# Moving four of the last output-projection products behind the last V pair, and splitting the copy of the last output half between ScalarE and VectorE

## The chip, the cores and the metric

One core of one Trainium2 chip. The metric is the device time of one execution in microseconds (us), median of several runs; lower is better. "Span" is the time from the first to the last instruction in a profile; the device time is some 2 us longer.

## The reference, cut to what matters

One decode step of an attention block over a KV cache, mixed by a gate with a small feed-forward block.

```python
B, Sq, D = 4, 1, 1024;  H, Sk, Dh = 32, 8192, 128        # all bf16
q = (x @ wq) ...                                          # [B, H, 1, Dh]
p = softmax(einsum("bhqd,bhkd->bhqk", q, k_cache) * Dh ** -0.5)
o = einsum("bhqk,bhkd->bhqd", p, v_cache)
a = o.reshape(B, Sq, H * Dh) @ wo                         # wo: 4096 x 1024, 8 MB
b = x + (silu(x @ w_gate) * (x @ w_up)) @ w_down * sigmoid(x @ w_r)   # one token per batch
out = g * a + (1 - g) * b                                 # g = sigmoid(sum(x * gate_w)), out: 4 x 1024
```

The two caches are 268 MB each and everything is read once, so the kernel is one long read from HBM.

## The kernel before: the parts that matter

Heads are taken in 32 "pairs" of 8 MB, `d = 0..31`. All loads go through one ring of five 4 MB slots and are issued by SyncE (SP), in program order. The end of the program is what the change touches: the last V pair (`d = 31`), the eight 1 MB blocks of `wo`, and the output.

```python
def v_pair(d):                                     # cut
    ...                                            # the last pair comes in pieces: 2 x 2 MB, 4 x 1 MB
    for u in range(4 * RD):                        # 64 products of 512 columns
        for w in range(4):
            nc.tensor.matmul(o_ps[w // 2][row:row + NM, w % 2, :], ...)      # L579
    if tv == GV - 1:
        sum_up(d, g, t, b, h0)

def sum_up(d, g, t, b, h0):                        # cut: the branch for the last pairs
    half = [OS[:], turned(P, 4 * Dh, F32)]
    for w in range(2):
        nc.scalar.activation(out=half[w], in_=o_ps[0][:, w, :], ...)         # L615
    for w in range(2):
        nc.vector.scalar_tensor_tensor(out=half[w], in0=o_ps[1][:, w, :], ...)   # L617
    nc.vector.tensor_tensor(out=OS[:], in0=half[0], in1=half[1], op=ALU.add)     # L619
    # finish(), run later: 8 small products that transpose OS into "led"     # L625

def wo_block(g, r0=0, r1=FR, half=None):           # issues the load, returns the products
    ...
    nc.sync.dma_start(out=w[:, r0:r1]..., in_=wov[:, g, r0:r1]...)           # L432
    def use():
        for r in range(r0, r1):
            for n in range(NH) if half is None else [half]:
                mm_acc(n, LT[:, r, g, :], w[:, r, n * NB:(n + 1) * NB])      # L287, 512 columns
    return use

# the end of the program
        if (kind, d) == ("v", ND - 1):
            for g in range(2):
                wo_block(g)()                      # 16 products ahead of the last V pair
        if kind == "v":
            v_pair(d)
        if (kind, d) == ("v", ND - 2):
            o_rows(0, GE)                          # LT for the wo blocks up to GE
last = [wo_block(g) for g in range(2, 4)]
cuts = [(g, r, r + 2) for g in range(4, NWB - 1) for r in (0, 2)] + [(NWB - 1, r, r + 1) for r in range(FR - 1)] + [(NWB - 1, 3, 4, n) for n in range(NH)]
last += [wo_block(*cut) for cut in cuts]
flush_sums()
last.pop(0)()                                      # block 2
flush()                                            # the transposing products of the last pair (L625)
flush_late()
last.pop(0)()                                      # block 3
o_rows(GE, NWB)                                    # L419, L421
for use in last:                                   # blocks 4 to 7, in ever smaller pieces
    use()
res = [turned(Bn, NB) for _ in range(NH)]
nc.vector.tensor_copy(out=res[0], in_=acc(0))      # L684
nc.sync.dma_start(out=out2[:, 0:NB], in_=res[0])   # L685
nc.scalar.copy(out=res[1], in_=acc(1))             # L686
nc.scalar.dma_start(out=out2[:, NB:D], in_=res[1]) # L687
```

## Time and profile before

| | before |
|---|---|
| device time, first three runs | 1342.71, 1342.55, 1342.71 us |
| span | 1340.5 us |
| HBM read | 575.68 MB |
| last V piece landed | 1321.86 us |
| last wo piece landed | 1337.07 us |
| last wo product starts | 1337.12 us |
| last arrival of the output | 1339.45 us |

A transfer has landed when the last of its increments is in (16 for a load; the small output transfers show five); I read those times from the semaphore records of the trace. The lines that carry the reading are in the prediction; one more, the last V pair, which runs its 64 products without a wait:

```profile
1310.84 14.00 PE L579 MATMUL o_ps<-ring,PB 128*64 128x512 bf16 x64
```

How to read the lines: in a chain, "start, length, what"; in a timeline, the same with engine, source line and operation, and in brackets how long the engine was idle before and for whom it waited. PE is TensorE, PEld its weight loads, DVE VectorE, ACT ScalarE, SPq and ACTq the issue of a transfer by SyncE or ScalarE.

### The profile page before, as it was taken

Reading aid. Unit: us, or ns where it says so; the run is one execution under the profiler, and the core shown is the slowest. Engines: PE = TensorE matmul, PEld = TensorE weight load, DVE = VectorE, ACT = ScalarE, POOL = GpSimd, SP = SyncE. Lnnn points to the kernel's source line nnn. Section 1 sums busy time; section 2 is a strip of 40 time slices with the busy share of each in tenths; the row PEclk is TensorE's granted clock in tenths of the full one; section 3 lists DMA queues with packets and bytes.
Section 4 is the critical chain, followed back from the end, with each engine's and each line's share of the span. In section 5 each row is a group of like instructions: output and inputs, shape, how many; then the busy total and the mean of one; then the engine's idle time right before and its main releaser. Section 6 shows DMA issues by size and latency. Waiting matters only on the chain.

```text
span 1340.5 us, 6937 instructions
## 1 busy us (share of the span) xinstructions
PE 1065.4 (79%) x4654; PEld 141.1 (11%) x1422; DVE 638.4 (48%) x385; ACT 57.7 (4%) x58; POOL 66.5 (5%) x174
## 2 busy tenths in 40 slices
PE   2666877887778788787879778789697879889888
PEld 0101000001001010101001010101011011111111
DVE  2455988556544347554436256646145556100001
ACT  0000000100010000100010000100000000110000
POOL 2000000100010000100010000100001000100000
PEclk9787999898988998888989888889898989889889
DMA  9999999999999999999999999999999999999998
GB/s 415 433 436 435 437 434 427 435 432 430 437 433 429 441 427 427 440 432 432 437 431 431 432 437 438 425 432 427 438 436 438 430 422 434 434 430 429 428 427 346
DMA packets 15512, 576.14 MB, mean 430 GB/s; under 512 B 1740, under 2 KB 2004, under 8 KB 3170
## 3 DMA queue, kind: packets, MB, share of 16 engines
q1 hardware_dynamic: 15474, 575.69, 99.6%
q8 instruction: 24, 0.39, 0.1%
q14 instruction: 6, 0.05, 0.0%
q10 hardware_dynamic: 8, 0.00, 0.0%
HBM read 575.68 MB, written 0.01 MB: 429 GB/s over the span
## 4 chain that ended last, share of the span: by engine, by line
DMA 60%; DVE 23%; PE 14%; another core or an unknown queue 1%; issue 0%; ACT 0%; SPq 0%; DVEq 0%
DMA ring<-in_A_k_cache_dram 51%; DVE TB L494 21%; PE o_ps L579 9%; DMA ring<-in_A_v_cache_dram 8%; PE acc L287 2%; PE S_ps L499 2%; DVE OS L609 2%; DMA x<-in_gate_w_dram 2%; DVE mx L521 0%; PE o_ps L333 0%; PE S_ps L333 0%; PE led L625 0%; DVE PT L535 0%; ACT TB L530 0%
## 5 line engine op out<-in xcount | busy, mean ns | idle before, releaser
L494 DVE STREAM_TRANSPOSE TB<-ring 128x2048 uint32<-128x2048 uint32 x256 | 568.2, 2278 | 471.6 <-DMA ring<-in_A_k_cache_dram 464.6
L499 PE MATMUL S_ps<-TB,Z 128*128 128x512 bf16 x2048 | 531.3, 414 | 187.3 <-DVE TB L494 179.7
L579 PE MATMUL o_ps<-ring,PB 128*64 128x512 bf16 x2048 | 466.4, 390 | 45.7 <-DMA ring<-in_A_v_cache_dram 44.4
L499 PEld LDWEIGHTS <-Z 128*128 128x128 bf16 x512 | 52.9, 103 | 650.7 <-issue 650.7
L579 PEld LDWEIGHTS <-PB 128*64 128x64 bf16 x512 | 57.5, 112 | 447.0 <-issue 442.6
L617 DVE SCALAR_TENSOR_TENSOR OS<-o_ps,mE,OS 128x512 f32<-128x512 f32 x5 | 3.8, 751 | 136.7 <-ACT OS L615 136.7
L476 POOL COPY Z<-qa 32x4 bf16<-32x4 bf16 x128 | 25.6, 200 | 720.4 <-PE S_ps L499 695.0
L555 POOL COPY PB<-PT 32x1024 bf16<-32x1024 bf16 (+3 forms) x23 | 33.2, 1443 | 455.5 <-PE o_ps L579 350.1
L605 ACT ACTIVATE OS<-o_ps,mE 128x512 f32<-128x512 f32 x11 | 7.6, 687 | 673.4 <-PE o_ps L579 673.4
L553 ACT COPY PB<-PT 32x1024 bf16<-32x1024 bf16 (+3 forms) x21 | 30.3, 1442 | 22.5 <-PE o_ps L579 17.5
L609 DVE SCALAR_TENSOR_TENSOR OS<-o_ps,mE,OS 128x512 f32<-128x512 f32 x33 | 24.3, 737 | 1.5
L530 ACT ACTIVATE TB<-S_ps,mx 128x2048 bf16<-128x2048 f32 x4 | 7.9, 1967 | 321.4 <-DVE mx L527 321.4
L287 PE MATMUL acc<-ring,hT 128*4 128x512 bf16 x54 | 14.7, 444 | 5.4 <-ACT TB L530 5.4
L245 PE MATMUL S_ps<-identb,x 6*128 6x6 bf16 x8 | 0.6, 197 | 22.1 <-DMA x<-in_gate_w_dram 22.1
L333 PE MATMUL o_ps<-ring,xw 128*4 128x512 bf16 (+2 forms) x128 | 13.1, 496 | 5.2 <-DMA ring<-in_B_w_gate_dram 5.2
L287 PE MATMUL acc<-ring,LT 128*4 128x512 bf16 x64 | 14.6, 379 | 0.4 <-DVE LT L421 0.4
L625 PEld LDWEIGHTS o_ps<-selg,OS 128*128 128x128 f32 x88 | 11.5, 191 | 9.3 <-issue 8.9
L535 DVE STREAM_TRANSPOSE PT<-TB 128x2048 bf16<-128x2048 bf16 x4 | 9.2, 2312 | 6.4 <-ACT TB L530 6.4
L521 DVE TENSOR_REDUCE mx<-S_ps 128x1 f32<-128x2048 f32 x4 | 9.1, 2282 | 6.2 <-PE S_ps L499 6.2
L625 PE MATMUL o_ps<-selg,OS 128*128 128x8 f32 x88 | 10.5, 245 | 0.0
L615 ACT ACTIVATE OS<-o_ps,mE 128x512 f32<-128x512 f32 x5 | 3.4, 687 | 149.3 <-PE o_ps L579 149.3
L637 DVE SCALAR_TENSOR_TENSOR OT<-led,sgb,rinv 128x8 bf16<-128x8 f32 x5 | 1.2, 237 | 17.3 <-PE led L625 17.3
(83 smaller groups left out, 89.0 us busy)
## 6 DMA issues: line engine op xcount, KB each, us to landing
ring<-in_A_v_cache_dram SPq DMA_DIRECT2D x18, 4096.0 KB, 28.9
ring<-in_A_k_cache_dram SPq DMA_DIRECT2D x14, 4096.0 KB, 33.5
ring<-in_A_v_cache_dram SPq DMA_DIRECT2D x6, 2048.0 KB, 36.8
ring<-in_B_w_gate_dram SPq DMA_DIRECT2D x1, 7168.0 KB
ring<-in_B_w_up_dram SPq DMA_DIRECT2D x1, 7168.0 KB, 37.0
ring<-in_B_w_down_dram SPq DMA_DIRECT2D x1, 6912.0 KB
ring<-in_A_wo_dram SPq DMA_DIRECT2D x4, 1024.0 KB, 32.5
ring<-in_A_v_cache_dram SPq DMA_DIRECT2D x4, 1024.0 KB, 36.0
```

The costliest lines, as they stand in the source:

```text
L287: nc.tensor.matmul(acc(n), lhsT=lhsT, rhs=rhs, start=start, stop=True, skip_group_check=True)
L333: nc.tensor.matmul(ps[32 * k:32 * k + Bn, z, :].rearrange("p (f r) -> p f r", r=FR)[:, :, lo:hi], lhsT=xT[TW * half + t], rhs=rhs, start=( ...
L476: nc.gpsimd.tensor_copy(out=Z[at, :, QP - 1 + QP * q], in_=qa[at, :, h0 + q, b])
L494: nc.vector.transpose(out=flat_t.bitcast(U32).rearrange("p (j i) -> p j i", j=CJ), in_=kn[:, half].bitcast(U32))
L499: nc.tensor.matmul(sps[:, z, :], lhsT=Z[:, 2 * half + e, s:s + P], rhs=T[:, 16 * z:16 * z + 16, :, e], start=(t + n + half + e == 0), stop ...
L521: nc.vector.tensor_reduce(out=mx[:, 0:1], in_=sps[:].rearrange("p z n -> p (z n)"), axis=AX.X, op=ALU.max)
L535: nc.vector.transpose(out=PT[:].rearrange("p j i -> p (j i)"), in_=PTs)
L553: nc.scalar.copy(out=Bv[at, :, :, q, :], in_=Pv[at])
L555: nc.gpsimd.tensor_copy(out=Bv[at, :, :, q, :], in_=Pv[at])
L579: nc.tensor.matmul(o_ps[w // 2][row:row + NM, w % 2, :], lhsT=PB[:, RD * (d % NW) + n, z].rearrange("p w s j -> p (w s j)"), rhs=vn[:, j0 ...
L609: nc.vector.scalar_tensor_tensor(out=OS[:], in0=o_ps[w // 2][:, w % 2, :], scalar=mE[:, w:w + 1], in1=OS[:], op0=ALU.mult, op1=ALU.add)
L625: nc.tensor.matmul(oT, lhsT=OS[:, q * Dh:(q + 1) * Dh], rhs=selg[:, q].rearrange("p t s -> p (t s)"), start=(q == 0), stop=(q == 3), skip_ ...
```

## The change

The intent: fill the gap in which TensorE waits for the sums of the last V pair, with products that until then stood ahead of that pair; and let two engines share the copy of the output half that is ready last.

```diff
-        def use():
-            for r in range(r0, r1):
+        def use(lo=r0, hi=r1):
+            for r in range(lo, hi):
...
         if (kind, d) == ("v", ND - 1):
-            for g in range(2):
-                wo_block(g)()
+            wo_block(0)()
+            near = wo_block(1)
+            near(0, 2)
+            last = [lambda: near(2, FR)]
...
-    last = [wo_block(g) for g in range(2, 4)]
+    last += [wo_block(g) for g in range(2, 4)]
...
-    last.pop(0)()
+    for _ in range(2):
+        last.pop(0)()
...
-    res = [turned(Bn, NB) for _ in range(NH)]
+    NC = NB // 2
+    res = [turned(Bn, NB) for _ in range(3)]
     nc.vector.tensor_copy(out=res[0], in_=acc(0))
     nc.sync.dma_start(out=out2[:, 0:NB], in_=res[0])
-    nc.scalar.copy(out=res[1], in_=acc(1))
-    nc.scalar.dma_start(out=out2[:, NB:D], in_=res[1])
+    nc.scalar.copy(out=res[1][:, 0:NC], in_=acc(1)[:, 0:NC])
+    nc.vector.tensor_copy(out=res[2][:, 0:NC], in_=acc(1)[:, NC:NB])
+    nc.scalar.dma_start(out=out2[:, NB:NB + NC], in_=res[1][:, 0:NC])
+    nc.sync.dma_start(out=out2[:, NB + NC:D], in_=res[2][:, 0:NC])
```

## The prediction

> **What bounds the kernel now.** I began with the page, to see which resource is full from end to end.
>
> ```profile
> PE 1065.4 (79%) x4654; PEld 141.1 (11%) x1422; DVE 638.4 (48%) x385; ACT 57.7 (4%) x58; POOL 66.5 (5%) x174
> DMA  9999999999999999999999999999999999999998
> HBM read 575.68 MB, written 0.01 MB: 429 GB/s over the span
> ```
>
> No engine is full, but the DMA row is at nine tenths or more in 39 of 40 slices, so the kernel is a stream of 575.68 MB from HBM with compute beside it. A change at the end can only pay if it shortens what comes after the last bytes, or brings those bytes earlier. So the second view was the chain of waits, cut to the last 34 us.
>
> ```profile
> 1307.29 3.62 PE acc L287 x16
> 1310.91 13.51 PE o_ps L579 x62
> ...
> 1326.61 0.70 DVE OS L619
> 1327.31 0.04 issue
> 1327.35 1.06 PE led L625 x8
> 1328.41 1.82 PE acc L287 x8
> ...
> 1330.40 6.02 PE acc L287 x27
> 1336.42 0.04 issue
> 1336.46 1.05 PE acc L287 x4
> 1337.51 0.02 issue
> 1337.53 0.57 ACT TB L686
> ```
>
> Read alone, this says TensorE all the way: 16 wo products, the last V pair, ScalarE and VectorE summing it, the products that transpose the sum (L625), the other wo products, a copy. That reading invites the change. But a chain goes through the predecessor on the same engine when an engine hardly pauses, and can hide that a transfer paces it: the 0.04 us "issue" at 1336.42 is a small break. So I read TensorE's matmuls and weight loads, and the DMA issues, in order of time.
>
> ```profile
> 1327.35 1.06 PE L625 MATMUL led<-selg,OS 128*128 128x8 f32 x8 [0.70 <-DVE OS L619]
> 1334.75 0.08 PEld L287 LDWEIGHTS <-LT 128*4 128x4 bf16 x1 [0.38 <-issue]
> ...
> 1336.67 0.08 PEld L287 LDWEIGHTS <-LT 128*4 128x4 bf16 x1 [0.55 <-issue]
> 1328.21 0.33 SPq L432 DMA_DIRECT2D ring<-in_A_wo_dram  x1
> 1337.30 0.68 DVE L684 CAST TB<-acc 4x512 bf16<-4x512 f32 x1 [6.64 <-PE acc L287]
> 1337.53 0.57 ACT L686 CAST TB<-acc 4x512 bf16<-4x512 f32 x1 [11.82 <-PE acc L287]
> 1338.01 0.29 SPq L685 DMA_DIRECT2D out_dram<-TB  x1
> 1338.13 0.54 ACTq L687 DMA_DIRECT2D out_dram<-TB  x1
> ```
>
> The first line is the gap that the change aims at: TensorE waits for OS (0.70 us after the modelled end of the product before it; from issue to issue 0.86). Next come the weight loads, normally 0.35 us apart here; two gaps are longer, 0.38 and 0.55, and belong to products that wait for a wo piece. The piece issued at 1328.21 (the third row of the last block) has this landing time:
>
> ```profile
> ring<-in_A_wo_dram SPq DMA_DIRECT2D x1, 256.0 KB, 8.2
> ```
>
> 1328.21 + 8.2 = 1336.41, and the product that needs it starts at 1336.46. So the end is paced by DMA. In the trace's semaphore records, each of these transfers is complete when the last of 16 arrivals is in: first half of block 4 at 1328.15, second 1329.43; block 5 at 1330.70 and 1331.99; block 6 at 1333.25 and 1334.49; block 7 row by row at 1335.11, 1335.75, 1336.41, and its last row in halves at 1336.78 and 1337.07. Half a block comes every 1.25 us or so; its four products take 4 x 0.216 = 0.86 us. TensorE is faster than the stream and had caught up with it already at 1334.53, where it first had to wait (landing 1334.49).
>
> **What the Trainium skill says.** "TensorE: Matmul & The Clock Gate", section "Back-to-back issue gap", gives N/2.4 + 2.5 ns, 216 ns at N = 512; here successive products are 0.216 us apart, so it agrees, and I use 0.216. "VectorE: DVE Perf Modes", section on the TRN2 errata, gives PSUM to SBUF copies (120 + N)/0.96 ns on VectorE and (172 + N)/1.2 ns on ScalarE: 658 and 570 ns at N = 512, against 678 and 574 in the lines above. So the slopes hold, and a 256-column copy should take 678 - 256/0.96 = 411 ns on VectorE and 574 - 256/1.2 = 361 ns on ScalarE (estimates from that page and these rows). "PSUM — Partial Sum Buffer", section "PSUM bank collisions raise a hardware error", says two engines may not be on the same bank and quadrant at once, disjoint columns included, and that the compiler orders such instructions. The trace of before has one engine per bank here and can't show it, but the built order of the changed kernel does: VectorE's second copy waits for ScalarE. "DMA: Bandwidth & Descriptors", section "Anatomy of one DMA", puts some 2.0 us of fixed cost on a transfer, mostly completion. Measured here, from the issue's start to the last arrival: 1338.01 to 1339.28 and 1338.13 to 1339.45, so 1.27 us on SyncE's queue and 1.32 on ScalarE's. I use the measured ones.
>
> **The change, part 1: four products moved.** Nothing is added or removed on TensorE. Four of the eight products of wo block 1 go from ahead of the last V pair to behind it, 4 x 0.216 = 0.86 us.
> - The last V pair starts at about 1309.98 instead of 1310.84, if its data are there. They are: its first piece landed at 1307.02. The tightest is its last quarter, landed at 1321.86; its first product was the 57th, at 1310.84 + 56 x 0.216 = 1322.94, and would be at 1322.08. The slack falls from 1.08 to 0.22 us and just holds.
> - ScalarE and VectorE then sum 0.86 us earlier: OS is ready at 1327.31 - 0.86 = 1326.45.
> - The moved four products, then block 2's eight, fill TensorE to 1326.49: the gap is filled almost exactly, and L625 starts at 1326.5 instead of 1327.35. This is a real 0.85 us at that place.
> - Then the pieces. Block 3 (landed 1326.87) runs at about 1327.5 to 1329.2, the last output rows' products until 1329.3, block 4 at 1329.3 and 1330.2, block 5's first half at 1331.05 (landed 1330.70). Its second half could start at 1331.9 but lands at 1331.99: wait. Block 6 could start at 1332.9, lands at 1333.25: wait; its second half could start at 1334.15 and starts, as before, at 1334.53. From there on the two kernels coincide. The 0.85 us becomes three waits for DMA instead of one gap for VectorE.
>
> Do the pieces land earlier? Their issues wait for the transfer eight places ahead (SyncE's queue waited for transfers in all of its last issues), the order on SyncE is unchanged, and the DMA share is 1.0 until 1330. So no. Part 1: 0.0 us.
>
> **Part 2: the output.** Before: ScalarE copies the second half from 1337.53 to 1338.10, issues at 1338.13, last arrival 1339.45. After:
> - VectorE's first copy is unchanged, 1337.30 to 1337.98; its transfer lands at 1339.28.
> - ScalarE copies 256 columns, 1337.53 to 1337.89, and its transfer lands at 1337.92 + 1.32 = 1339.24: 0.21 earlier.
> - VectorE's second copy must wait for its own first (1337.98 at the latest) and for ScalarE (1337.89 + 0.03). Start about 1337.95, + 0.41 = 1338.36; SyncE issues at 1338.39, being free since 1338.30; + 1.27 = 1339.66.
> The last arrival is now this one: 1339.66 against 1339.45, 0.2 us later. The balance was meant to be better, but VectorE is the engine that is still busy with the other half, so it is given work that it starts 0.42 us after ScalarE could. The buffers of their own only avoid a false dependence that was not there.
>
> Sum: 0.0 + 0.2. 1342.71 + 0.2 = 1342.9.
>
> **The rivals.**
> 1. TensorE really sets the end and the 0.85 us carries through: 1342.71 - 0.85 + 0.2 = 1342.1. For it: the chain names TensorE alone. Against it: the start at 1336.46, 0.05 us after a landing.
> 2. The output copy gains what it was meant to: two queues issue in parallel and half copies are shorter, so the end follows ScalarE's 1339.24 or the untouched 1339.28, about -0.17: 1342.5. For it: VectorE's two neighbouring sums start 0.67 apart at 0.75 us each, so neighbours overlap by some 0.08. Against: even so the last half can't be copied before 1338.3.
> 3. The last V pair catches up with its data and TensorE stalls: the slack is only 0.22 us. Even a stall of 0.5 us leaves TensorE ahead of where it must be at 1334.53, so still 1342.9.
> 4. A collision or queue effect on the third output transfer, a second one on SyncE's queue: some 0.3 us more, 1343.2.
>
> **Range and chances.** All terms together lie between -0.85 and +0.5 us, and the three runs of before lie within 0.16 us. Runs of another session may shift by some tenths, so 1342.1 to 1343.6. Two per cent is 27 us, which nothing here can reach: within 2% is all but certain.
>
> **What would show it.** In the changed kernel's trace: L625 of the last pair starting about 0.85 us earlier with no idle ahead of it; longer gaps than 0.35 us between weight loads from block 5 on; the product on the third row of the last block still 0.05 us behind its landing; the second VectorE copy ending near 1338.36 and its transfer the last to land. Wrong would be: the last wo product earlier by more than 0.3 us with landings as they were, or the third output transfer landing before ScalarE's.

## The result, and the profile after

1343.09 us median of five runs (1342.89 to 1343.96), against 1342.71 us (1342.55 to 1342.99) for before: 0.38 us slower, the ratio 1.0004 with a 95% interval of 0.999 to 1.0018. Ratios are the mean time of one kernel's runs over that of the other's of the same rounds, so not quite the ratio of the medians. The number lies in the forecast range, and there is no gain, as forecast. The trace says which steps held.

The chain of waits of the changed kernel, last 34 us:

```profile
1307.61 21.05 DMA ring<-in_A_wo_dram
...
1328.72 8.19 DMA ring<-in_A_wo_dram
1336.91 0.04 issue
1336.96 0.82 PE acc L287 x3
1337.78 0.02 issue
1337.80 0.68 DVE TB L688
1338.48 0.35 DVE TB L691
```

Now the chain names what paced the end: two wo transfers, one after the other, and TensorE only for the last products. The third row of the last block landed at 1328.72 + 8.19 = 1336.91, the product that needs it started at 1336.96: the 0.05 us of before. This is no new bottleneck: in before the last 31 products took 7.10 us, against 6.85 without a wait (e12 below), so TensorE already lost 0.25 us to late pieces, in pauses too short for the chain to leave the engine.

The timeline of the changed kernel, the lines of the last V pair (L579), the transposing products and the wo products with a wait:

```profile
1307.88 3.64 PE L579 MATMUL o_ps<-ring,PB 128*64 128x512 bf16 x16
1312.48 7.07 PE L579 MATMUL o_ps<-ring,PB 128*64 128x512 bf16 x32 [0.97 <-DMA ring<-in_A_v_cache_dram]
1319.93 1.89 PE L579 MATMUL o_ps<-ring,PB 128*64 128x512 bf16 x8 [0.38 <-DMA ring<-in_A_v_cache_dram]
1322.42 1.89 PE L579 MATMUL o_ps<-ring,PB 128*64 128x512 bf16 x8 [0.60 <-DMA ring<-in_A_v_cache_dram]
1326.92 1.06 PE L625 MATMUL led<-selg,OS 128*128 128x8 f32 x8
1333.79 1.02 PE L287 MATMUL acc<-ring,LT 128*4 128x512 bf16 x4 [0.22 <-DMA ring<-in_A_wo_dram]
1335.01 2.98 PE L287 MATMUL acc<-ring,LT 128*4 128x512 bf16 x12 [0.20 <-DMA ring<-in_A_wo_dram]
```

The idle time ahead of L625 is gone and waits for wo pieces have come, as forecast. But the waits in the second to fourth line were not forecast: the last V pair waits for its own data. TensorE came to it at 1307.88 us, 2.96 us earlier than in before, and only 0.86 of that is the four products moved. The rest is, by the estimate below the windows, the clock. The same stretch of both kernels by windows (columns: stretch, its length, busy us of PE, PEld, DVE, ACT, POOL with instructions, granted TensorE clock, DMA share, GB/s), before first:

```profile
1285.00:1300.00 15.00, 12.47 (x43) 2.97 (x17) 1.25 (x3) 0.00 (x0) 0.00 (x0) 0.66 0.99 419
```

```profile
1285.00:1300.00 15.00, 11.94 (x52) 2.37 (x20) 0.24 (x1) 0.00 (x0) 0.00 (x0) 0.89 0.99 417
```

In before the clock was at half for 10.24 us from 1285.6, in the run of after for 3.41 us from 1287.4. The pair ahead of the last was then multiplied, at 0.43 us a product instead of 0.216, for 8.36 us of the stretch in before and 2.80 in after. Half of the difference is 2.78 us; less the 0.53 by which that pair began later in after, this estimate gives 2.25, where 2.10 are to be explained. The program is the same up to there, and either order had both lengths (below, 3.4 us in e6 in the old order and 10.2 in e7 in the new), so I take it for chance of the execution; what makes a stretch longer, no run shows. Its length and place decide how late TensorE comes to the last V pair.

The output, from the timeline of the changed kernel:

```profile
1337.80 0.68 DVE L688 CAST TB<-acc 4x512 bf16<-4x512 f32 x1 [7.58 <-PE acc L287]
1338.03 0.36 ACT L690 CAST TB<-acc 4x256 bf16<-4x256 f32 x1 [12.84 <-PE acc L287]
1338.42 0.54 ACTq L692 DMA_DIRECT2D out_dram<-TB  x1
1338.42 0.41 DVE L691 CAST TB<-acc 4x256 bf16<-4x256 f32 x1
1338.51 0.29 SPq L689 DMA_DIRECT2D out_dram<-TB  x1
1338.86 0.28 SPq L693 DMA_DIRECT2D out_dram<-TB  x1
```

VectorE's half starts at 1338.42, 0.03 us after ScalarE's ends and 0.62 after VectorE's own first copy began. In e5 below, where VectorE does both copies, the second begins 0.60 us after the first. So VectorE's own first copy alone would have held it up nearly as long; the order behind ScalarE costs 0.02 us at most. Its transfer goes out last. The arrivals: 1339.62 (ScalarE's), 1339.79 (first half), 1340.03 (VectorE's). So the last arrival is 2.46 us after the last wo landing (1337.57), against 1339.45 - 1337.07 = 2.38 in before.

To compare runs in which the stream ends at different times, the experiments below use such intervals inside one trace:

| run | half clock from 1284 us on | last V landing to L625 | last V landing to last wo product | last wo landing to last output |
|---|---|---|---|---|
| before | 10.2 us | 5.50 | 15.26 | 2.38 |
| after | 3.4 | 4.54 | 15.23 | 2.46 |
| e1_order_only | 6.8 | 4.54 | 15.27 | 2.39 |
| e2_output_only | 6.8 | 4.72 | 15.25 | 2.46 |
| e3_short_stream | 6.8 | 4.45 | 14.08 | - |
| e4_short_stream_order | 6.8 | 4.54 | 14.07 | - |
| e5_serial_copy | 10.2 | 5.51 | 15.22 | 2.79 |
| e6_late_short_old | 3.4 | 6.33 | 15.85 | - |
| e7_late_short_new | 10.2 | 8.20 | 17.72 | - |
| e8_late_old | 10.2 | 9.88 | 19.40 | 6.52 |
| e9_late_new | 3.4 | 5.23 | 15.22 | 2.39 |
| e10_after_again | 6.8 | 4.54 | 15.22 | 2.46 |
| e11_before_as_itself | 10.2 | 5.48 | 15.26 | 2.37 |
| e12_buffer_only | 10.2 | 6.43 | 15.95 | 3.10 |

(The stretch of half clock is the one around the pair ahead of the last; a second one after the last product is left out. In the short streams the last column has no meaning.)

Two figures of these traces help to read the table. L625 starts 2.90 us after the last product of the V pair in all eight traces of the old order (2.89 in e6) and 2.99 in all six of the new one: the sums on ScalarE and VectorE set it (in the new order the twelve products outlast them by 0.1), and products put in their shadow do not make it earlier. Only an earlier last V product does. And from L625 to the last wo product it is 9.52 us where TensorE never waits for a piece (e6, e7, e8, e12), while the stream lets that product start 15.2 us after the last V landing at the earliest. So, by these figures, TensorE sets the end only where L625 comes more than some 5.7 us after that landing.

### The profile page after: what moved, and what is told of

Read it like the earlier page. It is cut to its first block, busy times and chain, and to the rows that moved or that the text cites. A ratio compares the mean times of both kernels' runs of the same rounds, so it can differ in the third digit from the quotient of the medians.

```text
span 1341.1 us, 6881 instructions
## 1 busy us (share of the span) xinstructions
PE 1057.4 (79%) x4596; PEld 140.9 (11%) x1422; DVE 638.9 (48%) x386; ACT 57.5 (4%) x58; POOL 67.0 (5%) x174
## 4 chain that ended last, share of the span: by engine, by line
DMA 66%; DVE 23%; PE 10%; issue 0%; SPq 0%; ACT 0%; DVEq 0%
DMA ring<-in_A_k_cache_dram 51%; DVE TB L494 20%; DMA ring<-in_A_v_cache_dram 10%; PE o_ps L579 8%; DMA ring<-in_B_w_gate_dram 3%; DMA ring<-in_A_wo_dram 2%; DVE OS L609 2%; PE S_ps L499 1%; PE o_ps L333 1%; DVE PT L535 0%; DVE mx L521 0%; PE led L625 0%; PE acc L287 0%; DVE OS L617 0%; DVE OT L637 0%
## 5 line engine op out<-in xcount | busy, mean ns | idle before, releaser
L579 PE MATMUL o_ps<-ring,PB 128*64 128x512 bf16 x2048 | 464.0, 389 | 50.0 <-DMA ring<-in_A_v_cache_dram 48.6
L579 PEld LDWEIGHTS <-PB 128*64 128x64 bf16 x512 | 57.3, 112 | 450.0 <-issue 449.5
L625 PEld LDWEIGHTS o_ps<-selg,OS 128*128 128x128 f32 x88 | 11.5, 191 | 9.3 <-issue 8.8
L625 PE MATMUL o_ps<-selg,OS 128*128 128x8 f32 x88 | 10.5, 245 | 0.0
```

Source lines behind the costliest of these rows:

```text
L579: nc.tensor.matmul(o_ps[w // 2][row:row + NM, w % 2, :], lhsT=PB[:, RD * (d % NW) + n, z].rearrange("p w s j -> p (w s j)"), rhs=vn[:, j0 ...
L625: nc.tensor.matmul(oT, lhsT=OS[:, q * Dh:(q + 1) * Dh], rhs=selg[:, q].rearrange("p t s -> p (t s)"), start=(q == 0), stop=(q == 3), skip_ ...
```

## The experiments

**e1_order_only.** The new order with the old output:

```diff
 # after.py, with the output of before (cut)
+    res = [turned(Bn, NB) for _ in range(NH)]
+    nc.scalar.copy(out=res[1], in_=acc(1))
+    nc.scalar.dma_start(out=out2[:, NB:D], in_=res[1])
```

> Part 1 alone: four products of wo block 1 behind the last V pair, output copied as before. My theory (the end is paced by the landings of the wo pieces): the gap of TensorE ahead of the transposing products (L625) goes, 0.86 us are gained there and all of it is given back in waits for pieces from block 5 on, so the first product on the third row of the last block still starts 0.05 us after that row's landing, the interval from the last wo landing to the last output arrival stays at 2.38 us as in before, and the time is that of before within 0.2 us. Rival (TensorE and the sums set the end): 0.7 to 0.9 us faster than before. Rival (the order itself disturbs the stream, part of the 0.38 us that the change lost): 0.2 to 0.4 us slower.

Measured: 1343.08 us median (1342.38 to 1343.84, five runs), before 1342.65 (1342.48 to 1344.17, nine runs), ratio 1.0, 0.9987 to 1.0012. The last wo product starts 15.27 us after the last V landing and the output follows 2.39 us after the last wo landing: both as in before. Part 1 alone gains nothing at the end, as the theory has it; the 0.7 to 0.9 us of the first rival are not there. The medians differ by 0.43 us, but the means of the same runs by 0.04: medians of so few runs of this kernel don't resolve a third of a us.

**e2_output_only.** The old order with the new output (the diff above, its last part alone).

> Part 2 alone: the order of before, the last output half copied by ScalarE and VectorE. My theory: the whole loss of the change that is not noise is here; from the last wo landing to the last output arrival 2.46 us as in the changed kernel against 2.38 in before, so 0.1 to 0.2 us slower than before. Rival (all of the 0.38 us of the change comes from the copies and the third transfer): that interval is 0.3 to 0.4 us longer than in before, 2.7 us or more. Rival (the copies shared are faster, and the order was what cost): 0.1 to 0.2 us faster than before.

Measured: 1343.16 us median (1342.93 to 1343.92), ratio 1.0002, 0.9988 to 1.0016. The interval is 2.46 us, the number of the theory. The times lie 0.51 us above before by medians and 0.27 by means, more than the 0.1 to 0.2 of the theory; the end of this part says where the rest lies. There is a by-product: this run has the order of before and yet L625 begins 4.72 us after the last V landing, not 5.50. With 6.8 us of half clock TensorE came earlier to the last V pair: only 0.31 us behind the landing of its last piece, where in before it was 1.08. The idle time in the shadow of the sums is still there, but in two parts, 0.32 us ahead of block 2, which had not landed, and 0.31 ahead of L625.

**e3_short_stream.** Does the stream set the end, and by how much? The last two wo blocks are not loaded; their products read blocks 2 and 3 (wrong; the comparison with the reference passed all the same, so its tolerance does not see this part of the result).

```diff
         w = wo_home[home][:, at]
-        if half is None:
+        if g >= NWB - 2:
+            w = wo_home[0][:, at]
+        elif half is None:
```

> Wrong result on purpose: before, but the last two of eight wo blocks are not loaded; their products use blocks 2 and 3, which are there. The stream ends 2.1 MB earlier, with the second half of block 5 at about 1332.0 us, and no product is removed. My theory: 32 products from block 4 on then run without a wait, 32 x 0.216 us from 1330.18 us, so only the small waits of before go, and the time falls by just 0.2 to 0.3 us: before is only barely paced by the stream. If the end were paced by the stream alone, with TensorE far ahead, it would be 4 to 5 us faster. If TensorE alone set the end, exactly as before (0.0).

Measured: 1342.05 us median (1341.58 to 1343.71), ratio 0.9995, 0.9983 to 1.0008. By the interval, the last product starts 14.08 us after the last V landing instead of 15.26: 1.18 us earlier. My number, 0.2 to 0.3, was a miss: I had derived it from a TensorE made late by the clock in the trace of before. With less delay TensorE has about 1.2 us of room against the wo pieces. That the end moves earlier at all without a product removed shows that the wo pieces paced it. The timeline of e3 shows the order of before without the gap ahead of the transposing products:

```profile
1322.06 1.89 PE L581 MATMUL o_ps<-ring,PB 128*64 128x512 bf16 x8 [0.60 <-DMA ring<-in_A_v_cache_dram]
1324.55 1.89 PE L287 MATMUL acc<-ring,LT 128*4 128x512 bf16 x8 [0.61 <-DMA ring<-in_A_wo_dram]
1326.46 1.06 PE L627 MATMUL led<-selg,OS 128*128 128x8 f32 x8
```

(L581 and L627 are L579 and L625 of before.) The last V pair waits for its data, block 2 waits for its landing, and then the transposing products follow with no wait for the sums that the profile lists. The gap has not gone: it lies ahead of block 2 as a wait for data (0.61 us), and L625 starts 2.90 us after the last V product as in before.

**e4_short_stream_order.** e3 with part 1.

> Wrong result on purpose: the short stream of e3 with part 1 of the change (four products behind the last V pair), the output as before. My theory: with the pieces out of the way the 0.86 us that part 1 gains ahead of L625 now reach the end, but for one wait of about 0.1 us for block 5's second half: 0.7 to 0.85 us faster than e3, 0.9 to 1.1 us faster than before. Rival (part 1 gains nothing even ahead of the pieces, or loses elsewhere): the same as e3 within 0.2 us.

Measured: 1342.3 us median (1341.66 to 1342.83), ratio 0.9994, 0.9981 to 1.0006. L625 starts 4.54 us after the last V landing (4.45 in e3), the last product 14.07 (14.08). My expectation failed and the number is the rival's: even with the late wo pieces out of the way part 1 does not show its 0.86 us. The pair is not equally late, though (6.8 us of half clock in both, but 5.5 us later in e4), so it is no clean test. In the old order e4's last V pair would have come to its last piece 0.31 us after the landing, as e2's did, and L625 4.72 us after it; by this estimate part 1 gained 0.18 us there, and could gain nothing in an execution like e3, whose pair waits for its data without it. The failed expectation overturned a step of the prediction. The new theory: part 1 can only pay as far as TensorE comes so late to the last V pair that the pair runs without waiting for its data.

**e5_serial_copy.** How do the copies count at the end?

```diff
-    nc.scalar.copy(out=res[1], in_=acc(1))
-    nc.scalar.dma_start(out=out2[:, NB:D], in_=res[1])
+    nc.vector.tensor_copy(out=res[1], in_=acc(1))
+    nc.sync.dma_start(out=out2[:, NB:D], in_=res[1])
```

> The order of before; VectorE copies both output halves one after the other, both transfers from SyncE. It measures how far the copies carry through to the end. My theory (the last arrival follows the last copy one to one): VectorE's second copy starts 0.60 us after its first and takes 0.68, so the last arrival is 0.23 + 0.60 + 0.68 + 0.03 + 1.27 = 2.81 us after the last wo landing, against 2.38 in before and 2.46 in the changed kernel: 0.43 us more than before. Rival (the copies are hidden behind something else at the end): 2.4 to 2.5 us.

Measured: 1343.7 us median (1343.41 to 1344.08, four runs), before 1342.79, ratio 1.0007, 0.9992 to 1.0022. The interval is 2.79 us, 0.41 more than in before. The copies carry through one to one.

**e6 to e9: TensorE made late.** Sixteen extra products into an unused bank (a part of PSUM, the memory that takes TensorE's results) ahead of the last V pair, with the short stream (e6 old order, e7 part 1) and with all blocks (e8, e9).

```diff
+        if (kind, d) == ("v", ND - 1):
+            for k in range(16):
+                nc.tensor.matmul(A_ps[1][0:Bn, 0], lhsT=LT[:, 0, 0, :], rhs=wo_home[0][:, 0, k % FR, 0:NB],
+                                 start=True, stop=True, skip_group_check=True)
         if kind == "v":
             v_pair(d)
```

> Wrong result in its wo blocks 6 and 7, as in e3; in the order of before, with 16 extra products (3.45 us) that write an unused bank ahead of the last V pair, so that TensorE comes late to that pair, as a stretch of lowered clock would make it. My new theory (a part of the change pays only if the last V pair is paced by TensorE, not by its own data): the last V pair runs without a wait, the transposing products L625 start about 6.5 us after the last V landing (4.45 in e3), and the last wo product starts some 16.1 us after that landing (14.1 in e3). It is the pair of e7. Rival (the sums on ScalarE and VectorE or a transfer set L625 whatever TensorE does): 4.5 us still.

> e6 with four products of wo block 1 moved behind the last V pair. My new theory: now part 1 pays in full, L625 about 5.7 us and the last wo product about 15.2 us after the last V landing, 0.86 us less than in e6 for both. Rival (part 1 never pays): the same as e6.

> Before, with all wo blocks loaded and a right result, and the 16 extra products of e6 ahead of the last V pair. My new theory: TensorE, 2 us behind, sets the end instead of the stream: L625 6.5 us after the last V landing and the last wo product 16.1 us after it against 15.25 in before, so 0.8 us slower than before. Rival (the stream sets the end with room to spare): 15.25, no slower.

> e8 with four products of wo block 1 moved behind the last V pair (part 1 alone), output as before. My new theory: L625 5.7 us after the last V landing, and the last wo product back at the stream's pace, 15.2 to 15.3 us after it: some 0.8 us faster than e8, as fast as before. So part 1 is room for a late TensorE and nothing else. Rival (it pays nothing): as e8, 16.1.

Measured, medians of four runs: e6 1345.25, e7 1344.78, e8 1344.92, e9 1342.93 us; before 1342.79 in the rounds of e6 to e8 and 1342.96 in those of e9. Against the landing, e6 came near what was written (6.33 and 15.85 us), and e9 for the last product (15.22; its L625 at 5.23 was 0.5 us earlier than written). e7 (8.20 and 17.72) and e8 (9.88 and 19.40) came 2 to 4 us later: the clock was at half for 10.2 us in their profiled runs and for 3.4 in those of e6 and e9. The pairs can't be told apart by their landings, nor by their times (e8: 1343.33, 1343.57, 1346.27, 1346.79; e9: 1342.83, 1342.84, 1343.01, 1346.83: two groups 3 to 4 us apart in both).

What can be compared is the stretch on TensorE from the first wo product to L625, because the half clock had ended before it in all four. It is 23.51 and 23.52 us in the old order (e6, e8) and 22.75 in the new one (e7, e9). In all four the last V pair ran its 64 products in 13.62 us from first to last start, without a wait. So when TensorE is late, part 1 does gain: 0.76 us, which is the 0.86 of the four products less the 0.10 by which twelve products outlast the sums (last V product to L625 2.99 us, against 2.89). With 9.52 us from L625 to the last product in e6, e7 and e8, the 0.76 us reach the last product where TensorE sets the end (e7). The timelines of e8 and e9, e8 first:

```profile
1315.45 14.00 PE L579 MATMUL o_ps<-ring,PB 128*64 128x512 bf16 x64
1331.97 1.06 PE L625 MATMUL led<-selg,OS 128*128 128x8 f32 x8 [0.70 <-DVE OS L619]
1335.02 6.85 PE L287 MATMUL acc<-ring,LT 128*4 128x512 bf16 x31
```

```profile
1310.83 14.00 PE L579 MATMUL o_ps<-ring,PB 128*64 128x512 bf16 x64
1327.44 1.06 PE L625 MATMUL led<-selg,OS 128*128 128x8 f32 x8
1330.49 7.32 PE L287 MATMUL acc<-ring,LT 128*4 128x512 bf16 x31
```

In e8 the 31 wo products run without a wait (6.85 us) and TensorE sets the end, 4.2 us behind the last landing; in e9, with no gap ahead of L625, they wait for pieces again (7.32 us for the same 31), and the end is the stream's. (e8 and e9 differ by the clock as well as by the order, so their ends don't measure part 1.)

**e10_after_again.** The changed kernel, unchanged.

> The changed kernel once more, unchanged, for the size of the chance in its first 0.38 us. My theory: from the last wo landing to the last output arrival 2.46 us again, 0.08 more than before; the time of its runs spreads over 1 us or more as that of before does, because the stream itself ends earlier or later, and its median lies between 0 and 0.5 us above that of before. Rival (the 0.38 us are the change's own): its median 0.3 to 0.45 us above and its interval longer than 2.46.

Measured: 1343.19 us median (1343.01 to 1343.92), before 1342.96 (1342.58 to 1343.54), ratio 1.0003, 0.9989 to 1.0016; 2.46 us again. Its last wo landing was at 1337.27 us, 0.30 earlier than in the first trace of the same kernel.

**e11_before_as_itself.** The kernel before against itself, no edit.

> A control: the kernel before, not changed in a byte, in the place of a changed kernel. The changed kernel and its parts had medians 0.2 to 0.5 us over those of before, of which 0.08 is accounted for. My theory (the rest is chance in the stream and in the place of a run in its round): its median lies 0.2 us or more from that of the other runs of before, too, and the spread is 1 us or more. Rival (the rest belongs to the change): its median is within 0.1 us of theirs. The interval from the last wo landing to the last output arrival must be 2.38 us.

Measured: 1342.82 us median (1342.54 to 1343.41), the other runs of before 1342.84 (1342.57 to 1343.47), ratio 1.0, 0.9986 to 1.0013; 2.37 us. My expectation of an offset of 0.2 us failed: the place of a run in its round adds nothing, and the number is the rival's, by which the rest belongs to the change. But this trace of the unchanged kernel has its last wo landing at 1337.60 us, 0.53 later than the first one and as late as that of after (1337.57). So a stream that ends as late as in the first trace of after needs no change of the program.

**e12_buffer_only.** The third buffer alone.

```diff
-    res = [turned(Bn, NB) for _ in range(NH)]
+    res = [turned(Bn, NB) for _ in range(3)]
...
-    nc.scalar.copy(out=res[1], in_=acc(1))
-    nc.scalar.dma_start(out=out2[:, NB:D], in_=res[1])
+    nc.scalar.copy(out=res[2], in_=acc(1))
+    nc.scalar.dma_start(out=out2[:, NB:D], in_=res[2])
```

> Before, but ScalarE's output half is copied into the third buffer instead of the second: the buffers of their own alone, no instruction added or moved. My theory: nothing, 2.38 us from the last wo landing to the last output arrival, and a median that differs from that of before by no more than e11's does. Rival (a changed program shifts the stream): 0.3 us slower than e11.

Measured: 1343.14 us median (1342.71 to 1344.02), ratio 1.0003, 0.999 to 1.0015. That is 0.32 us above e11, the rival's number; but in the one execution that has a trace the stream was not later (last wo landing 1337.35), and what the other four did is not shown. The interval was 3.10 us instead of the 2.38 expected, a miss, but the cause is not the buffer. The last wo product started 0.76 us after the last landing (0.04 in before): the half clock, 10.2 us from 1288.3, had made TensorE late, and the copies took from the last product on what they take in before (2.34 us). The timeline of e12:

```profile
1328.59 1.06 PE L625 MATMUL led<-selg,OS 128*128 128x8 f32 x8 [0.70 <-DVE OS L619]
1331.63 6.85 PE L287 MATMUL acc<-ring,LT 128*4 128x512 bf16 x31
```

That is the picture of e8, without anything added: the old order has executions in which TensorE sets the end, here by about 0.7 us. This is where part 1 could pay at the end, by some 0.7 us (estimate: L625 at 6.43 less 0.76 is 5.67, just inside the 5.7 above); no paired run shows it, or how often such executions come.

**Where the third of a us is.** Over all runs whose span was listed, the changed kernel (e10 and the first five, ten runs) has a mean time of 1343.27 us and a mean span of 1341.08; before (39 runs) 1342.95 and 1340.96. So 0.32 us, of which 0.12 in the span and the other 0.20 outside it. Inside, 0.08 is the longer output. Outside: time less span averages 2.19 and 2.20 us in the two sets of after, 2.18 in e2 and 2.17 in e5, and 1.90 to 2.08 in every other kernel, 1.99 in before. The four are those in which SyncE issues two output transfers. What is done in that time no profile shows, so this goes together in 19 runs and is not an explained cause.

## Why the prediction was right or wrong

*The end is paced by the landings of the wo pieces.* Right. The product on the third row of the last block started 0.05 us after its landing in after as in before, and e3, with no product removed, ended 1.18 us earlier by the interval.

*Part 1 is worth 0.0 us at the end.* Right in the number (e1: 15.27 us against 15.26), and the reason given, that what is gained ahead of the wo pieces turns into waits for them, is what e9 shows. Two steps to it were wrong for the kernel as it runs.
- "The slack falls from 1.08 to 0.22 us and just holds": it did not. In after the last V pair waited 0.97, 0.38 and 0.60 us for its pieces, because TensorE came to it 2 us earlier, for a reason other than the change: 3.41 us of half clock instead of 10.24. The pair waited for its last piece in e1, e4 and e10, too.
- "This is a real 0.85 us at that place": 0.76, as e6 to e9 show, and only in an execution whose last V pair is paced by TensorE, for it is the last V product that must come earlier. How far TensorE was behind the landing of the last piece sets the most that can be gained. Of the six traces of the old order without extra products, before, e5 and e11 (1.07 to 1.10 us behind) and e12 (2.03) have room for the whole 0.86; e2 (0.31) has room for a third, e3 for nothing. So the step fits the trace it was taken from, and the mistake was to take that lateness of TensorE for fixed. The page's row of granted clocks only hints at it (its last three slices are 889 in before and 999 in after); the windows show it.

*The order of loads and the stream stay.* Nothing contradicts it: SyncE's order is the same, and the last wo landing of the unchanged kernel (1337.07 and 1337.60) spans that of the changed one (1337.57 and 1337.27).

*Part 2 costs 0.2 us.* Right in sign and mechanism: ScalarE's copy took 0.362 us (0.361 forecast), VectorE's 0.411 (0.411), VectorE began behind ScalarE as the built order said (its own first copy would have held it up as long, less 0.02 us), and its transfer was last. The size in the span was 0.08: the 256-column transfer took 1.17 us from issue to last arrival where I had put the 1.27 of the 512-column one, and VectorE's copy began 0.62 us after the first where I had put 0.65. The measured total, 0.32, came near the forecast only by luck, with 0.20 us outside the span that I had not foreseen.

*The rivals.* "TensorE sets the end" was false for this change's traced runs, and true for e6 to e8 and the traced run of e12. "The output copy gains" was false (e2: 2.46 us). "The pair catches up with its data" happened, and the last product still came at the stream's pace (15.23 us), as that rival said. "A second transfer on SyncE's queue" has the right neighbourhood: the extra 0.20 us goes with it, but outside the span.

*Readings that were off and change nothing.* The piece called "its last quarter" is the last eighth of the V pair (1 MB of 8). The 0.35 us between weight loads is idle time; their starts are 0.43 apart. From the last product ahead of the gap to L625 it is 1.07 us, 0.86 more than the usual step. "So the slopes hold" was read off one size; the 256-column copies of after then bore it out.

No kernel that loads everything clearly beat before: the sums, copies and waits that were tried at this end are worth tenths of a us in a stream that ends 0.5 us earlier or later by itself.

## What to carry to other kernels

Before filling a gap on an engine, ask what its end hangs on. Here it hung on the last V product, so moving work into the gap could pay only where it made that product earlier, and whether it did changed from one execution to the next: look at the granted clock ahead of it and at the landing times of what the engine consumes, in more than one trace. When a stream of loads sets the end, time gained ahead of its last pieces turns into waits for them; measure from the last landing, inside one trace, when the effect is smaller than the spread of the times. Splitting a last copy between two engines did not pay here, because the second engine, still busy with the other half, began 0.39 us after the first; a split with a free second engine was not tried.

## What the Trainium skill lacked or had wrong

- "DMA: Bandwidth & Descriptors", "Anatomy of one DMA", gives a fixed cost of some 2.0 us for transfers that GpSimd issues. I found no such figure for SyncE and ScalarE: their output transfers of 2 and 4 KB took 1.17 to 1.32 us from issue to last arrival here.
- "VectorE: DVE Perf Modes", the section on the TRN2 errata: its VectorE row for PSUM to SBUF gives 658 and 392 ns for 512 and 256 columns, measured 678 and 411, so 20 ns more; the ScalarE row, 570 and 357 ns, measured 574 and 362, holds.
- "TensorE: Matmul & The Clock Gate", "What's actually happening", has the half clock released after at least one busy window of some 3.4 us, by a window that runs freely, and calls the number of slow products run-variable. The stretches near the end were 3.41, 6.83 or 10.24 us, one to three such windows, in executions of programs that are equal up to there. The page does not say what makes it two or three.
- The same page, "Back-to-back issue gap": the prediction took only the formula from it. The section calls that the gap of an isolated product, too long for a stream of weight loads and products, for which it gives some 131 ns at N = 512. The stream here fits the formula and not the 131: 216 ns (64 products of the last V pair, 13.62 us from first to last start).
- No page has the 0.2 us of device time outside the span that came with a second output transfer from SyncE (2.17 to 2.20 us of time less span, against 1.90 to 2.08).
